# A tanh-gelu in one ScalarE instruction, and a layernorm moved from ScalarE to VectorE, in a four-layer attention and gated-MLP kernel

## The chip, the cores and the metric

The kernel runs on one core of a Trainium2 chip. The metric is device time in microseconds (us) of one execution. A core has TensorE (PE in the profile, with its weight loads as PEld), VectorE (DVE), ScalarE (ACT), GpSimd (POOL) and SyncE (SP), which starts the DMAs here. The engines run their own instruction streams and meet only at semaphores.

## The reference

The input is one sequence of 2048 tokens with 512 channels in bf16. Four residual layers follow each other: attention, gated MLP, attention, gated MLP, with the same two sets of weights.

```python
def _A_ref(x, wq, wk, wv, wo):           # 32 query heads of 16, one shared key and value head
    scores = einsum('bhqd,bkd->bhqk', q, k) * 16 ** -0.5
    o = einsum('bhqk,bkd->bhqd', softmax(scores), v)
    return o.reshape(B, S, 512) @ wo
def _B_ref(x, w_in, w_sp, b_sp, w_out):
    z = gelu_tanh(x @ w_in)              # 512 -> 1792
    z1, z2 = z[..., :896], layernorm(z[..., 896:])
    g = einsum('ts,bsf->btf', w_sp, z2) + b_sp[None, :, None]
    return (z1 * g) @ w_out
x = x + _A_ref(layernorm(x)); x = x + _B_ref(layernorm(x))
x = x + _A_ref(layernorm(x)); x = x + _B_ref(layernorm(x))
```

The gelu is the tanh approximation, and the layernorms have no gain or bias (eps 1e-5).

## The kernel before

Everything is written out by hand: `K.op(engine, function, waits, inc)` appends an instruction, or a run of matmuls, to that engine's list, so that each engine's order is the order in which Python emits. A wait becomes a wait on a semaphore count in front of the instruction.

**Prologue.** SP loads X (in four groups of tiles), the weights and `b_sp`. VectorE pads the weights (`wq_pad`, `wk_rep`, `wv_rep`), halves `w_out_r` in place (line 243, which waits for `wB`, the arrival of both MLP weights), clears `V_aug`, and then does the first layernorm.

**Attention** (`layer_A`). A loop over 512 units of four 128x512 score blocks: TensorE fills score banks (line 755), ScalarE takes three banks at a time through Exp into `P_ring` (line 774), TensorE multiplies by V, accumulating in PSUM over the 16 key tiles (line 797). Projections, transposes and the output product run as side tasks between them. The change doesn't touch this part.

**MLP** (`layer_B`). A layernorm in four chunks ends in `xnT`, 512 channels by 2048 tokens. Then comes what is called the gelu stage below: 60 items, 32 `z2` items (16 token tiles by two halves of 448 features) and then 28 `z1` items (128 features by 512 tokens). Each item is four matmuls into one of four PSUM banks (`pe_item`, lines 894 and 899) and a gelu in four steps that ping-pong between two engines:

```python
a0: ACT  ybuf  = Square(SQA * bank)            # line 932
d3: DVE  ybuf  = (ybuf + GELU_C) * bank        # line 941
a1: ACT  thbuf = Tanh(ybuf)                    # line 952
d4: DVE  out   = (thbuf + 1) * bank            # line 962, twice the gelu
```

The `LAG` loop emits them software-pipelined, one item apart. `d4` reads the bank last, so TensorE's item k waits for `d4` of item k-4. The result is twice the gelu; the halved `w_out_r` corrects this for `z1`, and 4 eps in place of eps for the normalised `z2`. For each token tile of `z2`, VectorE takes `bn_stats` of both halves (line 967) and `bn_aggr` (970), GpSimd makes the reciprocal deviation (971, 973), VectorE makes `nb2` (982), and ScalarE normalises the tile in place with Identity, scale and bias (985). `emit_norm` places the last two some six items behind.

After the stage, four passes follow: 7 groups of 16 matmuls with the transposed spatial weights (line 1050), each with two VectorE steps (1060, 1066), and 28 matmuls with `w_out_r` (1082) with the residual add (1088). The first group waits for `gelu_done`, the last item's gelu, and, matmul by matmul, for the normalised tiles.

Of the kernel before, what the change touches and what calls it, by code (L numbers as in the profile page):

```python
# [104 lines left out]
def bass_interleave_layers__grouped_kv_mqa__mixer_gmlp__prompt_kernel(  # L105
# [747 lines left out]
    def layer_B(layer_idx, x_waits):  # L853
# [69 lines left out]
        def step_a0(k):  # L923
# [4 lines left out]
            wl = [(S_pe, st["pe"][k])]  # L928
            if k >= NSLOT:
                wl.append((S_dve, st["d3"][k - NSLOT]))  # L930
                wl.append((S_act, st["a1"][k - NSLOT]))
# [3 lines left out]
        def step_d3(k):  # L935
            it = items[k]
            slot = k % NSLOT
            bk = bank32(slot)
            n = item_N(it)
            wl = [(S_act, st["a0"][k])]  # L940
            st["d3"][k] = K.op("dve", lambda e, slot=slot, bk=bk, n=n: e.scalar_tensor_tensor(  # L941
                ybuf[:, slot, 0:n], ybuf[:, slot, 0:n], GELU_C, bk[:, 0:n], op0=ALU.add, op1=ALU.mult),
                waits=wl, inc=S_dve)

        def step_a1(k):
            it = items[k]
            slot = k % NSLOT
            n = item_N(it)
            wl = [(S_dve, st["d3"][k])]
            if k >= NSLOT:  # L950
                wl.append((S_dve, st["d4"][k - NSLOT]))
            st["a1"][k] = K.op("act", lambda e, slot=slot, n=n: e.activation(  # L952
                thbuf[:, slot, 0:n], ybuf[:, slot, 0:n], ACTF.Tanh), waits=wl, inc=S_act)

        def step_d4(k):
            it = items[k]
            slot = k % NSLOT
            bk = bank32(slot)
            n = item_N(it)
            wl = [(S_act, st["a1"][k])]  # L960
# [178 lines left out]
```

## Time and profile before

| | |
|---|---|
| median of 2 runs | 2545.94 us (2543.81 to 2548.08) |
| the profiled execution's own time | 2543.34 us |
| its span from first to last instruction | 2541.3 us |
| mean granted TensorE clock | 0.658 of full speed |
| busy: PE, ACT, DVE, POOL | 1881.8, 2003.9, 577.0, 43.9 us |

Busy times are sums over the whole span, and a matmul's duration in the trace contains its pipeline, so a busy PE isn't PE at its peak; the start-to-start distance of matmuls is what counts. The span falls into six stretches: the prologue to about 52 us, attention to 1004 us, an MLP to 1280 us, attention to 2264 us, and an MLP to the end, with layernorms between them.

### The profile page before, as it was taken

To read this page: it belongs to the slowest core of one execution; us is meant where nothing else is said; L and a number is where in the kernel's file an instruction comes from. 1 tells how busy PE (TensorE), PEld (TensorE's weight loads), DVE (VectorE), ACT (ScalarE), POOL (GpSimd) and SP (SyncE) were. 2 spreads that over 40 slices of the span, in tenths; PEclk is the share of its full clock that TensorE was granted. 3 is DMA by queue.
4 is the path that set the end of the run, shared out by engine and by line. 5 is a ranking of instruction groups with operands and counts; after the bars stand their busy time and mean duration, and the time that the engine had idled before them with its cause. 6 is when DMAs were issued, how large, how long until landed. Compare 5 with 4: busy or idle time off the path is not lost.

```text
span 2541.3 us, 26575 instructions
## 1 busy us (share of the span) xinstructions
PE 1881.8 (74%) x11173; PEld 521.4 (21%) x11232; DVE 577.0 (23%) x1099; ACT 2003.9 (79%) x1639; POOL 43.9 (2%) x95
## 2 busy tenths in 40 slices
PE   2877777777777777469958777777777777764699
PEld 1223111111111111224422111111111111112244
DVE  4322100010001000794352101000100000018933
ACT  1999999999999997380039999999999999964700
POOL 0000000000000000110000000000000000001000
PEclk9998555555555555699979655555555555556999
DMA  3036000000000000201100000000000000011020
GB/s 119 1 86 164 1 1 1 1 1 1 1 1 1 1 1 1 67 1 34 34 1 1 1 1 1 1 1 1 1 1 1 1 1 1 1 33 34 1 83 18
DMA packets 60072, 43.82 MB, mean 17 GB/s; under 512 B 34864, under 2 KB 57264, under 8 KB 59952
## 3 DMA queue, kind: packets, MB, share of 16 engines
q1 hardware_dynamic: 59952, 42.11, 5.6%
q8 instruction: 88, 1.44, 0.2%
q14 instruction: 32, 0.26, 0.0%
HBM read 31.62 MB, written 10.49 MB: 17 GB/s over the span
## 4 chain that ended last, share of the span: by engine, by line
issue 34%; ACT 29%; PE 22%; DVE 14%; POOL 1%; DMA 0%; SPq 0%; another core or an unknown queue 0%; ACTq 0%
ACT P_ring L774 29%; PE ps_all L1050 8%; PE ps_all L755 4%; DVE ybuf L941 2%; PE ps_all L797 2%; PE ps_all L1082 2%; DVE oT_bf L814 2%; PE ps_all L716 2%; DVE ln_stats L277 2%; PE ps_all L664 1%; DVE z2n L962 1%; DVE z1c L962 1%; PE ps_all L303 1%; DVE st_59 L967 1%; DVE st_37 L967 1%
## 5 line engine op out<-in xcount | busy, mean ns | idle before, releaser
L774 ACT ACTIVATE P_ring<-ps_all 128x1536 bf16<-128x1536 f32 (+1 forms) x1366 | 1846.6, 1560 | 268.3 <-PE ps_all L755 267.8
L755 PE MATMUL ps_all<-qT_pad,kT_rep 32*128 32x512 bf16 x4096 | 776.6, 564 | 382.7 <-ACT P_ring L774 379.0
L797 PE MATMUL ps_all<-P_ring,V_aug 128*32 128x512 bf16 x4096 | 595.0, 570 | 2.1 <-ACT P_ring L774 2.1
L814 DVE CAST oT_bf<-ps_all 128x512 bf16<-128x512 f32 x64 | 44.3, 692 | 1422.0 <-PE ps_all L797 1421.8
L755 PEld LDWEIGHTS ps_all<-qT_pad,kT_rep 32*128 32x128 bf16 x4096 | 142.4, 98 | 991.7 <-ACT P_ring L774 936.4
L1050 PE MATMUL ps_all<-wspT,z2n 128*128 128x512 bf16 x878 | 196.8, 383 | 7.7 <-issue 6.8
L797 PEld LDWEIGHTS ps_all<-P_ring,V_aug 128*32 128x32 bf16 x4096 | 112.6, 100 | 415.8 <-issue 411.7
L932 ACT ACTIVATE ybuf<-ps_all 128x448 f32<-128x448 f32 (+1 forms) x120 | 66.0, 550 | 105.5 <-PE ps_all L894 105.5
L1050 PEld LDWEIGHTS ps_all<-wspT,z2n 128*128 128x128 bf16 x896 | 88.3, 99 | 115.3 <-issue 11.9
L894 PE MATMUL ps_all<-w_in_r,xnTB 128*128 128x448 bf16 x256 | 73.0, 424 | 40.1 <-DVE z2n L962 37.9
L941 DVE SCALAR_TENSOR_TENSOR ybuf<-ybuf,ps_all 128x448 f32<-128x448 f32 (+1 forms) x120 | 75.6, 630 | 6.4 <-ACT ybuf L932 6.4
L952 ACT ACTIVATE thbuf<-ybuf 128x448 bf16<-128x448 f32 (+1 forms) x120 | 71.2, 593 | 6.6 <-DVE ybuf L941 3.0
L664 PE MATMUL ps_all<-ident,oT_bf 128*128 128x128 bf16 x256 | 37.0, 295 | 51.3 <-DVE oT_bf L814 51.3
L899 PE MATMUL ps_all<-xnTB,w_in_r 128*128 128x512 bf16 x218 | 57.1, 382 | 18.6 <-DVE z1c L962 11.2
L1060 DVE TENSOR_TENSOR gtmp<-ps_all,bsp_bc 128x512 f32<-128x512 f32 x56 | 38.7, 692 | 124.9 <-PE ps_all L1050 124.9
L493 DVE CAST qT_pad<-ps_all 128x512 bf16<-128x512 f32 x60 | 41.5, 692 | 109.7 <-PE ps_all L488 109.7
L488 PE MATMUL ps_all<-xnTA,wq_pad 128*128 128x512 bf16 x224 | 59.8, 385 | 4.2 <-issue 1.9
L303 PE MATMUL ps_all<-ident,xnB 128*128 128x128 bf16 x128 | 15.1, 312 | 49.8 <-DVE xnB L292 49.8
L716 PE MATMUL ps_all<-wo_r,onT 128*128 128x512 bf16 x120 | 41.9, 481 | 12.8 <-DVE X L721 6.6
L277 DVE BATCH_NORM_STATS2 ln_stats<-X 128x6 f32<-128x512 bf16 x64 | 42.5, 664 | 0.2
L894 PEld LDWEIGHTS ps_all<-w_in_r,xnTB 128*128 128x128 bf16 x256 | 23.2, 109 | 89.5 <-DVE z2n L962 67.9
L282 POOL TENSOR_SCALAR ln_veps<-ln_mv 128x4 f32<-128x4 f32 (+1 forms) x12 | 2.8, 234 | 2221.0 <-DVE ln_mv L278 2221.0
(70 smaller groups left out, 720.3 us busy)
## 6 DMA issues: line engine op xcount, KB each, us to landing
wspT<-wspt_scratch SPq DMA_DIRECT2D x8, 2048.0 KB, 9.3
wsp_stage_21<-in_B_w_sp_dram SPq DMA_DIRECT2D x16, 512.0 KB, 3.9
wspt_scratch<-wspT_tile SPq DMA_DIRECT2D x16, 512.0 KB, 5.0
X<-in_A_x_dram SPq DMA_DIRECT2D x4, 512.0 KB, 5.6
out_dram<-X SPq DMA_DIRECT2D x16, 128.0 KB, 2.5
w_in_r<-in_B_w_in_dram SPq DMA_DIRECT2D x1, 1792.0 KB, 9.6
w_out_r<-in_B_w_out_dram SPq DMA_DIRECT2D x1, 896.0 KB, 10.8
wq_nat<-in_A_wq_dram SPq DMA_DIRECT2D x1, 512.0 KB, 8.3
```

Source lines behind the costliest of these rows:

```text
L277: v1 = K.op("dve", lambda e, t=t: e.bn_stats(ln_stats[:, t, :], X[:, t, :]), waits=xw_for(xw, t), inc=S_dloc)
L664: ins = e.transpose(side_bank16[:, qt * 128:(qt + 1) * 128], oT_bf[:, par, qt * 128:(qt + 1) * 128], ident[:])
L716: ins = e.matmul(side_bank32[:, 0:D], onT[:, par, c, qt * 128:(qt + 1) * 128], wo_r[:, c, :], start=(c == 0), stop=(c == 3))
L755: ins = e.matmul(bk[:, 0:QC], kT_rep[32 * j:32 * j + 32, kt * 128:(kt + 1) * 128], qT_pad[32 * j:32 * j + 32, hg, qc * QC:(qc + 1) * QC], ...
L774: return e.activation(P_ring[:, s0:s0 + n, :], bank32(b0, n).rearrange("p (k q) -> p k q", k=n)[:, :, 0:QC], ACTF.Exp, scale=DH ** -0.5)
L797: ins = e.matmul(pv_bank[32 * j:32 * j + 32, 0:QC], V_aug[:, kt, 32 * j:32 * j + 32], P_ring[:, slot, :], tile_position=(0, 32 * j), start ...
L814: v = K.op("dve", lambda e: e.tensor_copy(oT_bf[:, par, :], pv_bank[:, 0:QC]), waits=wl, inc=S_acc)
L894: ins = e.matmul(bk[:, 0:448], xnT[:, kd, t * 128:(t + 1) * 128], w_in_r[:, kd, FH + h * 448:FH + (h + 1) * 448], start=(kd == 0), stop=(k ...
L932: st["a0"][k] = K.op("act", lambda e, slot=slot, bk=bk, n=n: e.activation(ybuf[:, slot, 0:n], bk[:, 0:n], ACTF.Square, scale=SQA), waits=w ...
L941: st["d3"][k] = K.op("dve", lambda e, slot=slot, bk=bk, n=n: e.scalar_tensor_tensor(ybuf[:, slot, 0:n], ybuf[:, slot, 0:n], GELU_C, bk[:, ...
L952: st["a1"][k] = K.op("act", lambda e, slot=slot, n=n: e.activation(thbuf[:, slot, 0:n], ybuf[:, slot, 0:n], ACTF.Tanh), waits=wl, inc=S_act)
L1050: ins = e.matmul(bk[:, 0:TCW], z2n[:, sti, ft * 128:(ft + 1) * 128], wspT[:, wb, sti, :], start=(sti == 0), stop=(sti == NT - 1))
```

## The change

The four gelu steps become one ScalarE instruction that reads the PSUM bank and writes the result in bf16, with the activation function `Gelu_apprx_tanh`. TensorE's item k now waits for that instruction of item k-4. The factor of two is gone, and with it the halving of `w_out_r` in the prologue and the 4 eps. The product with `w_out_r` names `wB` in its waits. The tiles of `z2` are normalised by a VectorE `tensor_scalar` (subtract the mean, multiply by the reciprocal deviation), so that `nb2` goes. The buffers `ybuf` and `thbuf` go.

```diff
-        K.op("dve", lambda e: e.tensor_scalar(w_out_r[:], w_out_r[:], 0.5, None, op0=ALU.mult),
-             waits=[wB], inc=S_dve)
...
             if k >= NSLOT:
-                assert st["d4"][k - NSLOT] is not None
-                wl.append((S_dve, st["d4"][k - NSLOT]))
+                wl.append((S_act, st["a0"][k - NSLOT]))
...
-            st["a0"][k] = K.op("act", lambda e, slot=slot, bk=bk, n=n: e.activation(
-                ybuf[:, slot, 0:n], bk[:, 0:n], ACTF.Square, scale=SQA), waits=wl, inc=S_act)
+            st["a0"][k] = K.op("act", lambda e, bk=bk, n=n, oap=oap: e.activation(
+                oap, bk[:, 0:n], ACTF.Gelu_apprx_tanh), waits=[(S_pe, st["pe"][k])], inc=S_act)
...
-            vnb = K.op("dve", lambda e, t=t: e.scalar_tensor_tensor(nb2[:, t:t + 1], mv2[:, t, 0:1], -1.0, rstd2[:, t:t + 1],
-                                                                  op0=ALU.mult, op1=ALU.mult),
-                       waits=[(S_pool, vr2[t])], inc=S_dve)
-            vz2n[t] = K.op("act", lambda e, t=t: e.activation(z2n[:, t, :], z2n[:, t, :], ACTF.Identity,
-                                                              bias=nb2[:, t:t + 1], scale=rstd2[:, t:t + 1]),
-                            waits=[(S_dve, vnb)], inc=S_act)
+            vz2n[t] = K.op("dve", lambda e, t=t: e.tensor_scalar(z2n[:, t, :], z2n[:, t, :], mv2[:, t, 0:1], rstd2[:, t:t + 1],
+                                                                op0=ALU.subtract, op1=ALU.mult),
+                           waits=[(S_pool, vr2[t]), (S_dve, vm[t])], inc=S_dve)
+        for k in range(NIT + 2):
             while pending_norm and pending_norm[0][0] <= k:
                 emit_norm(pending_norm.pop(0)[1])
...
+            if k < NIT:
+                step_pe(k)
+            if 0 <= k - 1 < NIT:
+                step_gelu(k - 1)
+        gelu_done = (S_act, st["a0"][NIT - 1])
```

What stands in a row on the engines follows. In these rows sem13 is `S_dve`, sem14 `S_dloc` (VectorE to itself), sem15 `S_act`, sem16 `S_pe`, sem11 `S_pool`, sem17 and sem19 the score fills and the P.V products, sem5 the MLP weights; line numbers of the changed kernel are its own.

ScalarE in the first MLP, kernel before, a few items into the gelu stage:

```order
L932 ACTIVATE ybuf<-ps_all 128x448 [waits sem15,sem16]
L952 ACTIVATE thbuf<-ybuf 128x448 [waits sem13]
L932 ACTIVATE ybuf<-ps_all 128x448 [waits sem15,sem16]
L985 ACTIVATE z2n<-z2n,nb_41,rstd_40 128x896 [waits sem13]
L952 ACTIVATE thbuf<-ybuf 128x448
```

ScalarE in the changed kernel, from the last Exp of the first attention over the whole gelu stage to the first Exp of the second:

```order
L772 ACTIVATE P_ring<-ps_all 128x1024 [waits sem19,sem17]
L923 ACT_TABLE_LOAD
L923 ACTIVATE z2n<-ps_all 128x448 [waits sem16] x32
L923 ACTIVATE z1c<-ps_all 128x512 [waits sem16] x28
L772 ACT_TABLE_LOAD
L772 ACTIVATE P_ring<-ps_all 128x1536 [waits sem17] x4
```

ScalarE's stage is now 60 equal instructions that wait for TensorE alone. Four `ACT_TABLE_LOAD`s stand in the program (before each attention and each gelu stage), where before one stood at its start; the waits stand behind the loads, on the instruction that follows.

VectorE in the `z2` part of the stage, kernel before:

```order
L967 BN_STATS st_37<-z2n 128x6 [waits sem13]
L941 SCALAR_TENSOR_TENSOR ybuf<-ybuf,ps_all 128x448 [waits sem15]
L982 SCALAR_TENSOR_TENSOR nb_41<-mv_38,rstd_40 128x1 [waits sem11]
L962 SCALAR_TENSOR_TENSOR z2n<-thbuf,ps_all 128x448 [waits sem15]
L967 BN_STATS st_37<-z2n 128x6 [waits sem13]
L970 BN_AGGR mv_38<-st_37 128x2 [waits sem14]
```

The same place in the changed kernel:

```order
L930 BN_AGGR mv_36<-st_35 128x2 [waits sem14]
L927 BN_STATS st_35<-z2n 128x6 [waits sem15] x2
L930 BN_AGGR mv_36<-st_35 128x2 [waits sem14]
L942 TENSOR_SCALAR z2n<-z2n,mv_36,rstd_38 128x896 [waits sem13,sem11]
L927 BN_STATS st_35<-z2n 128x6 [waits sem15] x2
```

The four passes over each token tile's two halves are gone from between the statistics, and the normalisation of tile t stands behind the statistics of tile t+2. In the `z1` part VectorE has nothing left to do.

VectorE in the prologue, kernel before, from the last weight padding on:

```order
L220 MEMSET wv_rep 128x256
L239 COPY wv_rep<-wv_nat 128x16x16 [waits sem13]
L243 TENSOR_SCALAR w_out_r<-w_out_r 128x3584 [waits sem5]
L220 MEMSET V_aug 128x1024
L220 MEMSET V_aug 128x64 [waits sem13]
```

In the changed kernel:

```order
L220 MEMSET wv_rep 128x256
L239 COPY wv_rep<-wv_nat 128x16x16 [waits sem13]
L220 MEMSET V_aug 128x1024
L220 MEMSET V_aug 128x64 [waits sem13]
L275 BN_STATS ln_stats<-X 128x6 [waits sem0]
```

No wait for the MLP weights stands in front of the first layernorm any more.

## Rows read from the trace of the kernel before

**Rows 1.** Windows by stage: busy us per engine (count), granted clock, DMA share, GB/s.
```profile
52.50:1004.20 951.70, 728.34 (x4788) 178.85 (x4803) 106.06 (x186) 923.43 (x683) 0.00 (x0) 0.60 0.07 17
1052.26:1149.21 96.95, 65.15 (x238) 20.35 (x242) 91.40 (x184) 78.03 (x136) 12.66 (x32) 0.90 0.00 1
1149.21:1280.00 130.79, 122.82 (x549) 54.80 (x560) 50.38 (x73) 0.00 (x0) 0.00 (x0) 0.99 0.10 33
1309.00:2264.30 955.30, 729.03 (x4532) 163.28 (x4547) 83.99 (x155) 923.13 (x683) 0.00 (x0) 0.57 0.00 1
2312.39:2409.34 96.95, 64.89 (x238) 20.28 (x241) 91.42 (x184) 78.02 (x136) 12.66 (x32) 0.90 0.00 0
```

**Rows 2.** Timeline, z1 part: start, us, engine, line, shapes, idle before and releaser.
```profile
1143.51 0.58 ACT L932 ACTIVATE ybuf<-ps_all 128x512 f32<-128x512 f32 x1
...
1143.59 1.04 PE L899 MATMUL ps_all<-xnTB,w_in_r 128*128 128x512 bf16 x4 [0.16 <-DVE z1c L962]
1144.05 0.68 DVE L962 SCALAR_TENSOR_TENSOR z1c<-thbuf,ps_all 128x512 bf16<-128x512 bf16 x1
1144.17 0.63 ACT L952 ACTIVATE thbuf<-ybuf 128x512 bf16<-128x512 f32 x1
...
1144.70 0.58 ACT L932 ACTIVATE ybuf<-ps_all 128x512 f32<-128x512 f32 x1
```

**Rows 3.** Timeline, one item of the z2 part on TensorE.
```profile
1071.99 0.93 PE L894 MATMUL ps_all<-w_in_r,xnTB 128*128 128x448 bf16 x4 [0.99 <-DVE z2n L962]
```

**Rows 4.** Timeline: first weight loads at full clock in either gelu stage, then line 1050's.
```profile
1057.09 1.07 PEld L894 LDWEIGHTS ps_all<-w_in_r,xnTB 128*128 128x128 bf16 x6 [0.22 <-issue]
...
2316.47 1.51 PEld L894 LDWEIGHTS ps_all<-w_in_r,xnTB 128*128 128x128 bf16 x8 [0.22 <-issue]
...
1152.83 21.90 PEld L1050 LDWEIGHTS ps_all<-wspT,z2n 128*128 128x128 bf16 x102 [0.15 <-issue]
...
2412.25 1.82 PEld L1050 LDWEIGHTS ps_all<-wspT,z2n 128*128 128x128 bf16 x9 [0.25 <-issue]
```

**Rows 5.** Timeline, VectorE behind two neighbouring groups of 16 matmuls of line 1050.
```profile
1158.00 0.69 DVE L1060 TENSOR_TENSOR gtmp<-ps_all,bsp_bc 128x512 f32<-128x512 f32 x1 [2.03 <-PE ps_all L1050]
...
1161.45 0.69 DVE L1060 TENSOR_TENSOR gtmp<-ps_all,bsp_bc 128x512 f32<-128x512 f32 x1 [2.04 <-PE ps_all L1050]
```

**Rows 6.** Groups by line: busy us, mean ns of one, idle before and releasers.
```profile
L941 DVE SCALAR_TENSOR_TENSOR ybuf<-ybuf,ps_all 128x448 f32<-128x448 f32 (+1 forms) x120 | 75.6, 630 | 6.4 <-ACT ybuf L932 6.4
...
L952 ACT ACTIVATE thbuf<-ybuf 128x448 bf16<-128x448 f32 (+1 forms) x120 | 71.2, 593 | 6.6 <-DVE ybuf L941 3.0
...
L932 ACT ACTIVATE ybuf<-ps_all 128x448 f32<-128x448 f32 (+1 forms) x120 | 66.0, 550 | 105.5 <-PE ps_all L894 105.5
...
L962 DVE SCALAR_TENSOR_TENSOR z2n<-thbuf,ps_all 128x448 bf16<-128x448 bf16 x64 | 39.3, 613 | 0.0
L962 DVE SCALAR_TENSOR_TENSOR z1c<-thbuf,ps_all 128x512 bf16<-128x512 bf16 x56 | 38.2, 682 | 1.3 <-ACT thbuf L952 1.1
...
L967 DVE BATCH_NORM_STATS2 st_37<-z2n 128x6 f32<-128x448 bf16 x32 | 20.1, 627 | 1.1
...
L985 ACT ACTIVATE z2n<-z2n,nb_41,rstd_40 128x896 bf16<-128x896 bf16 x16 | 18.1, 1133 | 11.7 <-DVE nb_41 L982 11.6
...
L292 DVE TENSOR_SCALAR xnB<-X,ln_mv,ln_rstd 128x512 bf16<-128x512 bf16 x32 | 11.1, 409 | 11.8 <-POOL ln_rstd L284 11.8
...
L970 DVE BATCH_NORM_AGGREGATE mv_38<-st_37 128x2 f32<-128x12 f32 x16 | 3.3, 208 | 0.6
```

**Rows 7.** Timeline, prologue: the table load, and VectorE around the halving of w_out_r.
```profile
0.72 1.28 ACT L774 ACT_TABLE_LOAD   x1 [0.72 <-PEq L1124]
...
14.58 0.23 DVE L239 COPY wv_rep<-wv_nat 128x256 bf16<-128x256 bf16 x1
20.14 1.09 DVE L243 TENSOR_SCALAR w_out_r<-w_out_r 128x3584 bf16<-128x3584 bf16 x1 [5.34 <-DMA w_out_r<-in_B_w_out_dram]
21.40 0.91 DVE L220 MEMSET V_aug<- 128x1024 uint32 x1 [0.16 <-issue]
```

More of the change, by code (lines that the diff above doesn't have):

```diff
@@ L874, in layer_B @@
         rstd2 = K.sb([P, NT], FP32, lst, name="rstd2")
-        nb2 = K.sb([P, NT], FP32, lst, name="nb2")
         items = []
@@ L908, in out_ap @@
             return z1c[:, ft, tc * TCW:(tc + 1) * TCW]
-        st = {"pe": [None] * NIT, "a0": [None] * NIT, "d3": [None] * NIT, "a1": [None] * NIT, "d4": [None] * NIT}
+        st = {"pe": [None] * NIT, "a0": [None] * NIT}
         vm = [None] * NT
@@ L918, in step_pe, with step_gelu @@
             if k >= NSLOT:
[L919 to L920 removed]
+                wl.append((S_act, st["a0"][k - NSLOT]))
             st["pe"][k] = K.op("pe", lambda e, it=it, bk=bk: pe_item(e, it, bk), waits=wl, inc=S_pe)
[L923 removed]
+        def step_gelu(k):
             it = items[k]
@@ L927, in step_a0 @@
             n = item_N(it)
[L928 to L931, printed above, removed]
-            st["a0"][k] = K.op("act", lambda e, slot=slot, bk=bk, n=n: e.activation(
-                ybuf[:, slot, 0:n], bk[:, 0:n], ACTF.Square, scale=SQA), waits=wl, inc=S_act)
[L935 to L960, printed above, removed]
             oap = out_ap(it)
-            st["d4"][k] = K.op("dve", lambda e, slot=slot, bk=bk, n=n, oap=oap: e.scalar_tensor_tensor(
-                oap, thbuf[:, slot, 0:n], 1.0, bk[:, 0:n], op0=ALU.add, op1=ALU.mult),
-                waits=wl, inc=S_dve)
+            st["a0"][k] = K.op("act", lambda e, bk=bk, n=n, oap=oap: e.activation(
+                oap, bk[:, 0:n], ACTF.Gelu_apprx_tanh), waits=[(S_pe, st["pe"][k])], inc=S_act)
             if it[0] == "z2":
@@ L967, in step_d4 @@
                 v1 = K.op("dve", lambda e, t=t, h=h: e.bn_stats(st2[:, t, h, :], z2n[:, t, h * 448:(h + 1) * 448]),
-                          waits=[(S_dve, st["d4"][k])], inc=(S_dloc if h == 1 else None))
+                          waits=[(S_act, st["a0"][k])], inc=(S_dloc if h == 1 else None))
                 if h == 1:
                     vm[t] = K.op("dve", lambda e, t=t: e.bn_aggr(mv2[:, t, :], st2[:, t, :, :]), waits=[(S_dloc, v1)], inc=S_dve)
-                    vp1 = K.op("pool", lambda e, t=t: e.tensor_scalar(veps2[:, t:t + 1], mv2[:, t, 1:2], 4.0 * LN_EPS, None,
+                    vp1 = K.op("pool", lambda e, t=t: e.tensor_scalar(veps2[:, t:t + 1], mv2[:, t, 1:2], LN_EPS, None,
                                                                        op0=ALU.add), waits=[(S_dve, vm[t])], inc=S_ploc)
@@ L1008, in layer_B @@
             emit_norm(pending_norm.pop(0)[1])
-        z2n_all = (S_act, max(vz2n))
+        z2n_all = (S_dve, max(vz2n))
         wspT = K.sb([P, 2, NT, TCW], BF16, lst, name="wspT")
@@ L1048, in pe_g @@
                         if first_g:
-                            e.wait_ge(S_act.h, vz2n[sti])
+                            e.wait_ge(S_dve.h, vz2n[sti])
                         ins = e.matmul(bk[:, 0:TCW], z2n[:, sti, ft * 128:(ft + 1) * 128], wspT[:, wb, sti, :],
@@ L1054, in layer_B @@
                     wl = [w_ for w_ in wl if w_ is not z2n_all]
-                    K.waited["pe"][id(S_act)] = max(K.waited["pe"].get(id(S_act), 0), vz2n[NT - 1])
+                    K.waited["pe"][id(S_dve)] = max(K.waited["pe"].get(id(S_dve), 0), vz2n[NT - 1])
                 vg = K.op("pe", pe_g, waits=wl, inc=S_pe)
@@ L1074, in layer_B @@
                 bk = bank32(6 + yb)
-                wl = [(S_dve, vh[NF1 - 1]), w_prep]
+                wl = [(S_dve, vh[NF1 - 1]), w_prep, wB]
                 if y_bank_free[yb] is not None:
```

16 lines of the change are left out of this document (removed).

## The prediction

> **What bounds the kernel now.** I read the windows by stage first, to see which stretches the change can touch at all [rows 1]. The two attention stretches (951.7 and 955.3 us) have ScalarE busy for 923 us each, all of it Exp, and the change leaves their instructions as they are. The two gelu stages take 96.95 us each, and there VectorE is busy for 91.4, ScalarE for 78.0, and TensorE has 65 us in a duration that contains its pipeline. So VectorE bounds this stage. The stretch behind it (130.8 us) is TensorE's, at a granted clock of 0.99.
>
> The timeline shows how [rows 2]. In the z1 part one item starts every 1.19 us (ScalarE's Square at 1143.51 and again at 1144.70). VectorE's last step at 1144.05 follows the one of the item before, ScalarE's Square and Tanh (0.58 and 0.63) fill the same 1.19 us, and TensorE's four matmuls start only when VectorE releases the bank [rows 2]. In the z2 part TensorE stands idle for 0.99 us in front of an item that takes it 0.93 [rows 3], because VectorE also has the statistics to do. So the question for the change is what is late next once VectorE's two passes are gone: TensorE or ScalarE.
>
> **TensorE's own pace.** Neighbouring groups of 16 matmuls at full clock are 1161.45 - 1158.00 = 3.45 us apart [rows 5], 0.2158 us for one of 512 columns, with the wait at a group's head inside it. By columns, one of 448 takes 0.1888 us. The stage has 32 x 4 = 128 of the shorter and 28 x 4 = 112 of the longer: 24.17 + 24.17 = 48.3 us. At the start the clock is at the lower of its two levels (1.2 against 2.4 GHz): after 52 us with little on TensorE, weight loads come at the fast distance only from 1057.09 and 2316.47 on [rows 4], 4.8 and 4.1 us behind the starts of the stages [rows 1]. In that time TensorE does half of what it could, which costs 2.4 and 2.0 us.
>
> **ScalarE's pace.** An item is one activation out of PSUM. The nearest rows are Square from PSUM (mean 0.550 us) and Tanh (0.593) [rows 6]; no row shows `Gelu_apprx_tanh`. From below I take Square; from above, Square and Tanh one behind the other, 1.19 us. I take 0.58, Square's time at 512 columns [rows 2], since this too is one pass over PSUM. An item then takes TensorE 0.76 or 0.86 us and ScalarE 0.55 or 0.58, so ScalarE waits, a bank is free again more than an item before its turn (four banks), and TensorE runs without a gap.
>
> **VectorE's pace.** Per token tile two `bn_stats` (0.627), one `bn_aggr` (0.208) and the moved normalisation. For that last one, the row of line 292 is the same operation on the same types: 0.409 us for 512, hence at most 0.716 for 896 by columns [rows 6]; ScalarE's own pass over the tile took 1.133, the upper end. So 2.18 us per tile, 34.9 us for 16, from about 1055 to 1090. It is slower than TensorE's 1.51 us per tile, but TensorE no longer waits for VectorE in the stage, and 28 z1 items (24 us) lie behind the tiles. That is the cover: the first matmul of line 1050 needs the normalised tiles, and they are ready some 14 us earlier. Nothing of VectorE's is on the path.
>
> **The stage's end.** From an item's first matmul to ScalarE's start is 1144.70 - 1143.59 = 1.11 us [rows 2], that is 0.25 behind the fourth matmul's slot; then 0.58 for the gelu and 0.06 for the release: 0.9 us. A stage is 48.3 + 2.4 + 0.9 = 51.6 us, and 51.2 in the second MLP, in place of 96.95: **45.3 and 45.7 us less**.
>
> **Behind the stage.** Before, TensorE sat idle for 3.4 us while the last items went through four steps, and line 1050's first matmuls ran at the lower clock: full distance only from 1152.83 and 2412.25 on [rows 4], 3.6 and 2.9 us after their start. With a gap of 0.9 us I expect the clock to stay, which gives back half of that: **1.8 and 1.5 us**.
>
> **The prologue.** VectorE finishes the padding at 14.81 and then waits 5.3 us for the `w_out_r` transfer; `V_aug` is cleared only from 21.40 [rows 7], and the whole chain to the first Exp hangs behind that on VectorE. Without the halving it starts at 14.84: **6.6 us less**. X was loaded ahead of these weights on the same queue, so the layernorm's inputs aren't late next. SP's first loads of `w_sp` wait for the same `V_aug` and move forward too; they now run beside the rest of the weights, whose first user is the MLP, a millisecond later.
>
> **Edits at nothing.** The 4 eps, `nb2`, the buffers and the doubled `wB` change no time. The program has four table loads in place of one. The load shown takes 1.28 us and ran at 0.72 us, while its Exp waited until 52 us [rows 7, 1]: it isn't held by that wait. The order of the changed kernel has the waits behind the load in all four places, so each runs in ScalarE's idle time between the stages (over 50 us ahead of a gelu stage). I cost them at nothing; on the path the three more would cost 3 x 1.28 = 3.8 us. By the Trainium skill, "ScalarE: Activation LUTs", "What ACT_TABLE_LOAD costs", a switch of sets is about 2.66 us with its drain; as an estimate from that page, three on the path would cost 8 us, and the time would be 2453. No row here shows the drain.
>
> **The sum.** 45.3 + 45.7 + 1.8 + 1.5 + 6.6 = 100.9 us. The profiled execution took 2543.3 us, 2.0 more than its span, and would take 2442.4; the median of the runs lies 2.6 above that execution, so the forecast is **2445 us**, 4% less.
>
> **Rivals.**
> *ScalarE becomes the bound.* If the gelu costs what Square and Tanh cost together, an item takes 1.19 us at 512 and 1.07 at 448, the stage 28 x 1.19 + 32 x 1.07 + 2 = 69.6 us, and the kernel 2545.9 - 2 x 27.4 - 6.6 = 2485 us. It decides from 0.86 us per gelu on. For it: no row shows the function. Against: Square and Tanh, different functions, differ by 8% [rows 6].
>
> *The normalisation is late.* With ScalarE's 1.133 for a tile and GpSimd's whole 12.66 us of the stage [rows 1] in series, VectorE needs 16 x 2.60 + 12.7 = 54.2 us, 5 more than it has: 2445 + 10 = 2455. It decides above 3 us per tile. Against: GpSimd's part of a tile has two further tiles' statistics to hide behind.
>
> *The clock doesn't hold.* Before, the stage was granted 0.90 on average [rows 1], with TensorE idle for up to half of an item. If it stays at that, 48.3 / 0.90 = 53.7 us: 3.2 more per stage than I have, and the 3.3 us behind the stages are lost: 2455. At the lower level throughout, 95.6 us, the stage would gain nothing: 2539, within 2%. For it the Trainium skill has a rule, "TensorE: Matmul & The Clock Gate", "A second HAM failure mode: psum-queue depth-cycling": a kernel that cycles through PSUM banks leaves TensorE short idle times between groups, and its clock swings between the two levels. Against it stands the stretch of line 1050, which also cycles through its banks: 0.99 [rows 1].
>
> *Slower than before.* The mechanism is that the chip evaluates `Gelu_apprx_tanh` at the price of the steps that it replaces: 0.550 + 0.630 + 0.593 + 0.645 = 2.42 us [rows 6], all on ScalarE. A stage is then 60 x 2.42 + 1.8 = 147 us, 50 more than before, and the kernel 2545.9 + 100 - 6.6 = 2639 us. It decides from 1.64 us per gelu, three times the Square. Against it: Exp, too, takes one pass here. The Trainium skill, "ScalarE: Activation LUTs", "Step-by-step: what each stage is for", has one element per cycle and lane whatever the function; no run here shows that for this one.
>
> *The change does nothing that it says.* That is excluded: the order shows one activation per item and no VectorE pass left.
>
> **How the numbers follow.** The forecast's case 0.82, table loads on the path 0.03 (2449), the normalisation 0.03 (2455), the clock 0.05 (2455, of which 0.01 for 2539), ScalarE 0.05 (2485), slower 0.02 (2639). For the range: downward, no slow start at all gives 4.4 us more, and the two attention stretches differ by 3.6 us with the same work [rows 1], which is what a shifted start may change; with the spread of the two runs (2 us) that is 2435. Upward, the loads, the normalisation and the clock reach 2455, and with the same spreads 2460. What lies outside is ScalarE, slower and the clock's far end, under 0.1, and the tails. Two per cent, about what a measurement of this kernel can tell from no change, is 2495: faster 0.95 (it takes in most of ScalarE's case), same 0.03, slower 0.02.
>
> **What would show it.** In the changed profile: 60 activations of about 0.53 and 0.58 us per stage, ScalarE idle before each because of TensorE, line 894's matmuls 0.19 us apart without waits for a bank; the stage some 51 us long; line 1050 starting 0.9 us behind the last matmul at full clock; the last normalised tile some 14 us before that; the first Exp near 46 us; table loads inside idle time. Wrong: a gelu above 0.86 us, weight loads that wait for ScalarE, a granted clock below 0.9 in the stage, or attention stretches that changed by more than 4 us.

## The result, and the profile after

The changed kernel takes **2444.38 us** (median of 2 runs, 2443.28 to 2445.48) against 2545.94 before: a ratio of 0.9601, 95% interval 0.956 to 0.9642. The profiled execution took 2443.28 us with a span of 2441.3, that is 100.0 less span than before. The mean granted clock is 0.649.

The windows by stage of the changed kernel, with the columns of [rows 1]:

```profile
46.50:997.40 950.90, 729.30 (x4782) 180.21 (x4796) 105.46 (x185) 923.61 (x683) 0.00 (x0) 0.60 0.07 17
1047.13:1099.50 52.37, 51.48 (x242) 24.49 (x246) 27.15 (x64) 35.14 (x61) 15.02 (x32) 0.96 0.00 1
1099.50:1228.00 128.50, 120.21 (x546) 53.88 (x555) 50.69 (x75) 0.27 (x1) 0.00 (x0) 1.00 0.10 33
1257.00:2210.00 953.00, 726.85 (x4527) 163.32 (x4540) 84.01 (x154) 923.40 (x684) 0.00 (x0) 0.57 0.00 1
2259.60:2312.00 52.40, 51.47 (x244) 24.54 (x248) 27.15 (x64) 34.13 (x60) 15.02 (x32) 0.97 0.00 1
```

The second and fifth rows are the gelu stages. VectorE's work in one has fallen from 91.4 to 27.2 us and ScalarE's from 78.0 to some 34, and the stage now has TensorE's length. The attention rows have the same ScalarE work as before (923 us).

The groups by line of the changed kernel that answer to [rows 6] (shapes apart; the last number but one is the mean in ns, then the idle time before):

```profile
L889 PE MATMUL ps_all<-w_in_r,xnTB 128*128 128x448 bf16 x256 | 52.7, 371 | 1.6 <-DVE xnTB L309 1.6
L894 PE MATMUL ps_all<-xnTB,w_in_r 128*128 128x512 bf16 x218 | 48.0, 379 | 0.3
L923 ACT ACTIVATE z2n<-ps_all 128x448 bf16<-128x448 f32 x64 | 34.8, 544 | 115.8 <-PE ps_all L889 115.8
L923 ACT ACTIVATE z1c<-ps_all 128x512 bf16<-128x512 f32 x56 | 33.4, 597 | 15.0 <-PE ps_all L894 15.0
L942 DVE TENSOR_SCALAR z2n<-z2n,mv_36,rstd_38 128x896 bf16<-128x896 bf16 x16 | 7.5, 476 | 0.5 <-POOL rstd_38 L933 0.5
```

One gelu takes 0.544 or 0.597 us, and every idle time of ScalarE before one is TensorE's. TensorE itself has no idle time that ends with a bank's release: no "<-ACT" stands in its two rows, where [rows 3] showed 0.99 us of waiting for one item.

The timeline of the changed kernel, both ends of the first gelu stage and the start of the second (start, length, engine; the idle time before and its releaser in brackets):

```profile
997.45 1.28 ACT L923 ACT_TABLE_LOAD   x1
...
1047.13 6.11 PE L889 MATMUL ps_all<-w_in_r,xnTB 128*128 128x448 bf16 x20 [0.79 <-DVE xnTB L309]
...
1051.56 1.42 PEld L889 LDWEIGHTS ps_all<-w_in_r,xnTB 128*128 128x128 bf16 x8 [0.20 <-issue]
...
1078.75 0.51 DVE L942 TENSOR_SCALAR z2n<-z2n,mv_36,rstd_38 128x896 bf16<-128x896 bf16 x1 [0.46 <-POOL rstd_38 L933]
1078.88 0.60 ACT L923 ACTIVATE z1c<-ps_all 128x512 bf16<-128x512 f32 x1 [0.27 <-PE ps_all L894]
1079.74 0.60 ACT L923 ACTIVATE z1c<-ps_all 128x512 bf16<-128x512 f32 x1 [0.27 <-PE ps_all L894]
...
1097.87 0.60 ACT L923 ACTIVATE z1c<-ps_all 128x512 bf16<-128x512 f32 x1 [0.27 <-PE ps_all L894]
1098.49 1.28 ACT L772 ACT_TABLE_LOAD   x1
1098.54 4.44 PEld L999 LDWEIGHTS ps_all<-wspT,z2n 128*128 128x128 bf16 x22 [1.20 <-issue]
1098.57 4.69 PE L999 MATMUL ps_all<-wspT,z2n 128*128 128x512 bf16 x21 [0.73 <-issue]
1102.22 0.69 DVE L1009 TENSOR_TENSOR gtmp<-ps_all,bsp_bc 128x512 f32<-128x512 f32 x1 [22.96 <-PE ps_all L999]
...
2263.30 1.61 PEld L889 LDWEIGHTS ps_all<-w_in_r,xnTB 128*128 128x128 bf16 x9 [0.18 <-issue]
```

One z1 item starts every 0.86 us, 1.19 in [rows 2]. The stage runs from 1047.13 to line 999's first matmul at 1098.57, 51.44 us. Line 999 (1050 before) runs at full clock from its first weight load, where [rows 4] had it 3.6 us later. Its first VectorE step follows 3.65 us behind the first matmul. The last tile is normalised at 1079.26, 19 us before line 999 needs it. Both table loads stand in ScalarE's idle time. The second stage lasts from 2259.64 to 2310.70, 51.06 us.

VectorE in the prologue and the first Exp, in the timeline of the changed kernel, for [rows 7]:

```profile
14.64 0.23 DVE L239 COPY wv_rep<-wv_nat 128x256 bf16<-128x256 bf16 x1
15.02 0.91 DVE L220 MEMSET V_aug<- 128x1024 uint32 x1 [0.16 <-issue]
...
46.95 1.45 ACT L772 ACTIVATE P_ring<-ps_all 128x1536 bf16<-128x1536 f32 x1 [44.95 <-PE ps_all L753]
```

### The profile page after: what moved, and what is told of

Its sections match the earlier page's. It is cut to its first block, busy times and chain, and to the rows that moved or that the text cites. A ratio compares the mean times of both kernels' runs of the same rounds, so it can differ in the third digit from the quotient of the medians.

```text
span 2441.3 us, 26105 instructions
## 1 busy us (share of the span) xinstructions
PE 1850.9 (76%) x11173; PEld 530.3 (22%) x11232; DVE 447.6 (18%) x858; ACT 1920.4 (79%) x1490; POOL 48.6 (2%) x95
## 4 chain that ended last, share of the span: by engine, by line
issue 35%; ACT 29%; PE 26%; DVE 7%; POOL 1%; DMA 0%; SPq 0%; another core or an unknown queue 0%; ACTq 0%; DVEq 0%
ACT P_ring L772 29%; PE ps_all L999 8%; PE ps_all L753 4%; PE ps_all L795 2%; PE ps_all L889 2%; PE ps_all L1031 2%; PE ps_all L894 2%; DVE oT_bf L812 2%; PE ps_all L714 2%; DVE ln_stats L275 2%; PE ps_all L662 1%; PE ps_all L301 1%; DVE X L719 1%; PE ps_all L696 1%; POOL ln_rstd L282 1%
## 5 line engine op out<-in xcount | busy, mean ns | idle before, releaser
L923 ACT ACTIVATE z2n<-ps_all 128x448 bf16<-128x448 f32 x64 | 34.8, 544 | 115.8 <-PE ps_all L889 115.8
L889 PE MATMUL ps_all<-w_in_r,xnTB 128*128 128x448 bf16 x256 | 52.7, 371 | 1.6 <-DVE xnTB L309 1.6
L894 PE MATMUL ps_all<-xnTB,w_in_r 128*128 128x512 bf16 x218 | 48.0, 379 | 0.3
L923 ACT ACTIVATE z1c<-ps_all 128x512 bf16<-128x512 f32 x56 | 33.4, 597 | 15.0 <-PE ps_all L894 15.0
L662 PEld LDWEIGHTS ps_all<-ident,oT_bf 128*128 128x128 bf16 x256 | 21.2, 127 | 81.8 <-DVE oT_bf L812 81.8
L383 PE MATMUL ps_all<-xnTA,wk_rep 128*128 128x512 bf16 x26 | 9.3, 484 | 34.2 <-DVE xnTA L309 34.2
```

Of the source, the lines that this page charges most:

```text
L662: ins = e.transpose(side_bank16[:, qt * 128:(qt + 1) * 128], oT_bf[:, par, qt * 128:(qt + 1) * 128], ident[:])
L889: ins = e.matmul(bk[:, 0:448], xnT[:, kd, t * 128:(t + 1) * 128], w_in_r[:, kd, FH + h * 448:FH + (h + 1) * 448], start=(kd == 0), stop=(k ...
L894: ins = e.matmul(bk[:, 0:TCW], w_in_r[:, kd, ft * 128:(ft + 1) * 128], xnT[:, kd, tc * TCW:(tc + 1) * TCW], start=(kd == 0), stop=(kd == K ...
L923: st["a0"][k] = K.op("act", lambda e, bk=bk, n=n, oap=oap: e.activation(oap, bk[:, 0:n], ACTF.Gelu_apprx_tanh), waits=[(S_pe, st["pe"][k]) ...
```

## The experiments

The kernel before, run beside each, had medians of 2544.1 to 2545.1 us. A stage runs from the first matmul with `w_in_r` to the first one with `wspT`. "Changed" is the changed kernel, 51.44 and 51.06 us per stage.

**What bounds the stage before: the normalisation alone moved (e3).** The kernel before with only this edit:

```diff
-            vz2n[t] = K.op("act", lambda e, t=t: e.activation(z2n[:, t, :], z2n[:, t, :], ACTF.Identity,
...
+            vz2n[t] = K.op("dve", lambda e, t=t: e.tensor_scalar(z2n[:, t, :], z2n[:, t, :], mv2[:, t, 0:1], rstd2[:, t:t + 1],
```

> The kernel before with its four gelu steps, and the second layernorm's tiles normalised on VectorE: the other half of the change alone. Theory (VectorE's work bounds the stage before): about 0.4 us more and 0.1 less of VectorE per tile, 16 x 0.3 = 5 us more per stage, 102 us in place of 96.95, about 2556. Rival (the relay between ScalarE and VectorE bounds it, and ScalarE loses 1.13 us per tile): the stage gets shorter, by 5 us or more, 2536 or less.

Measured: 2554.55 us (2551.64 to 2556.65), ratio 1.0038 (1.0025 to 1.0051); stages 102.36 and 101.96 against 96.95. The window over the first stage shows VectorE (the third pair) busy for nearly all of it:

```profile
1052.00:1156.00 104.00, 70.81 (x242) 21.98 (x246) 97.71 (x185) 64.04 (x120) 12.70 (x32) 0.84 0.00 0
```

The stage grew by 5.4 us as VectorE's work in it did by 5.7 (of the 97.71, 0.66 is a copy of the layernorm just ahead of the stage), although ScalarE lost 14: VectorE bound the z2 part, where the normalisation stands. The run doesn't decide the z1 part, which it leaves alone: there both engines were near full before (VectorE 26.5 and ScalarE 25.4 of the 27 us from 1118 to 1145). The second half of the change, alone, makes the kernel slower by 0.4%.

**The other half alone: gelu in one step, normalisation left on ScalarE (e2).** The changed kernel, with `nb2` again.

```diff
-            vz2n[t] = K.op("dve", lambda e, t=t: e.tensor_scalar(z2n[:, t, :], z2n[:, t, :], mv2[:, t, 0:1], rstd2[:, t:t + 1],
...
+            vz2n[t] = K.op("act", lambda e, t=t: e.activation(z2n[:, t, :], z2n[:, t, :], ACTF.Identity,
```

> The changed kernel, with the second layernorm's tiles normalised on ScalarE again (Identity, 1.13 us per tile). Theory: ScalarE then needs 2 x 0.54 + 1.13, about 2.1 us per tile with overlap, against TensorE's 1.51, so that it bounds the z2 part: 16 x 0.6 = 9 to 10 us more per stage, about 2463. Rival (ScalarE's idle time and the four banks take it up): under 2 us per stage, at most 2448. Second rival (Identity needs another table): two loads of 1.28 us per tile, over 40 us more per stage.

Measured: 2484.86 us (2483.68 to 2485.77), ratio 0.9765 (0.9749 to 0.9782); stages 71.84 and 71.51, 20.4 more each, twice what was expected. ScalarE's added work is 16 x 1.133 = 18 us, and in the first row of the changed stage above it had 52.4 - 35.1 = 17 us idle. The next two runs ask what the rest is.

**The same, with the normalisation 12 items behind (e11).**

```diff
-                    pending_norm.append((k + 6, t))
+                    pending_norm.append((k + 12, t))
```

> The changed kernel with the normalisation left to ScalarE as before (Identity, nb2 by VectorE), each placed 12 items behind its statistics in place of 6. If what cost 20 us per stage in the earlier version was the relay in order (ScalarE waits for nb, which stands behind statistics that wait for gelus), then with the wait gone only ScalarE's work counts: 0.85 us for two gelus and 1.13 for the normalisation against TensorE's 1.51 per tile, some ten tiles inside the z2 part: 5 to 8 us more per stage than the changed kernel, stage 57 to 60, 2456 to 2461. If it is the work on ScalarE and its wait on VectorE anyhow: 71 per stage, 2484 again.

Measured: 2477.13 us (2476.15 to 2480.13), ratio 0.9739 (0.9724 to 0.9754); the first stage 68.15. A miss (2456 to 2461 was expected): the greater distance takes away 7.7 us of e2's 40.5, and the wait only where no statistics are left. One tile of the z2 part in its timeline, and two rows of the z1 part:

```profile
1071.93 1.13 ACT L946 ACTIVATE z2n<-z2n,nb,rstd 128x896 bf16<-128x896 bf16 x1 [1.05 <-DVE nb L943]
...
1072.97 0.96 ACT L924 ACTIVATE z2n<-ps_all 128x448 bf16<-128x448 f32 x2
1073.52 1.15 DVE L928 BATCH_NORM_STATS2 st<-z2n 128x6 f32<-128x448 bf16 x2 [1.63 <-ACT z2n L924]
...
1074.71 0.21 DVE L931 BATCH_NORM_AGGREGATE mv<-st 128x2 f32<-128x12 f32 x1
1074.84 0.11 DVE L943 SCALAR_TENSOR_TENSOR nb<-mv,rstd 128x1 f32<-128x1 f32 x1
1074.98 1.13 ACT L946 ACTIVATE z2n<-z2n,nb,rstd 128x896 bf16<-128x896 bf16 x1 [1.05 <-DVE nb L943]
...
1092.22 1.13 ACT L946 ACTIVATE z2n<-z2n,nb,rstd 128x896 bf16<-128x896 bf16 x1
1093.25 1.08 ACT L924 ACTIVATE z1c<-ps_all 128x512 bf16<-128x512 f32 x2
```

The `nb` of an old tile, whose inputs have long been there, stands in VectorE's order behind the statistics of the two gelus that ScalarE has just made; ScalarE's Identity waits for `nb`, and the next gelus stand behind Identity. The two engines run in turn, 3.05 us per tile, with 12 items of distance as with 6 (e2). In the z1 part the same Identity waits for nothing.

**The same, with nb made ahead (e13).** VectorE's `nb` six items earlier than the Identity.

```diff
+                    pending_nb.append((k + 6, t))
...
+            while pending_nb and pending_nb[0][0] <= k:
+                emit_nb(pending_nb.pop(0)[1])
```

> The version with the normalisation on ScalarE placed 12 items behind, with one difference: VectorE makes nb of a tile six items earlier than ScalarE's Identity needs it, so that it stands ahead of, not behind, the statistics that wait for ScalarE's last gelus. The relay's account: the wait of 1.05 us in front of each Identity goes; a tile in the z2 part takes ScalarE 0.95 + 1.04 = 2.0 us against TensorE's 1.51, one in the z1 part 2.0 against 1.73, as the z1 part of the earlier version already showed; ten tiles in the one and six in the other give 10 x 0.47 + 6 x 0.25 = 6 us more per stage than the changed kernel: stage 57 to 58, 2456 (2453 to 2460). If the Identity's own work on ScalarE or another wait cost the 16 us of that version: 2477 again.

Measured: 2451.71 us (2449.27 to 2454.28), ratio 0.9636 (0.962 to 0.9652); the first stage 55.49, 4.1 more than changed where 6 were expected. ScalarE in its timeline:

```profile
1061.85 1.14 ACT L951 ACTIVATE z2n<-z2n,nb,rstd 128x896 bf16<-128x896 bf16 x1
...
1062.88 0.98 ACT L924 ACTIVATE z2n<-ps_all 128x448 bf16<-128x448 f32 x2
...
1063.72 1.15 ACT L951 ACTIVATE z2n<-z2n,nb,rstd 128x896 bf16<-128x896 bf16 x1
```

The wait is gone, and a tile takes 1.87 us, not the 2.0 expected. Of e2's 40.5 us, 8 went with the distance (e11), 25 with the order of `nb` on VectorE, and some 7 are left for ScalarE's work. So the moved normalisation is worth 7 us with the best order tried here, and 40 with the order that the kernel before had.

**Does ScalarE bound the changed stage? A small extra activation per item (e5).** 32 columns more, 0.20 us by its duration.

```diff
+            K.op("act", lambda e, bk=bk, n=n, slot=slot: e.activation(
+                gscr[:, slot, 0:32], bk[:, 0:32], ACTF.Gelu_apprx_tanh), waits=[(S_pe, st["pe"][k])])
```

> The changed kernel with one extra gelu of 32 columns per item into a scratch tile, about 0.2 us of ScalarE. Theory (TensorE bounds): 0.54 + 0.2 and 0.60 + 0.2 us stay under TensorE's 0.757 and 0.863 per item, so the stage stays within 1 us of 51.3 and the time within 3 us of the changed kernel's. Rival (ScalarE's time or latency adds to each item): 0.2 x 60 = 12 us more per stage, about 2468.

Measured: 2442.49 us (2442.14 to 2444.79), ratio 0.9601 (0.9588 to 0.9614); stages 51.72 and 51.62, 0.3 and 0.6 more. The gelu behind the extra one starts 0.09 us after it, so by start distances 60 x 0.09 = 5.4 us were added per stage, and not 12; nearly all of it is hidden, and the kernel isn't slower. ScalarE doesn't bound the stage; with no wait in TensorE's rows either, TensorE does.

**Every gelu twice (e4).** The same edit with all columns.

```diff
+                gscr[:, slot, 0:n], bk[:, 0:n], ACTF.Gelu_apprx_tanh), waits=[(S_pe, st["pe"][k])])
```

> The changed kernel with every gelu computed twice, the first into a scratch tile that nobody reads. Theory (TensorE bounds the stage, ScalarE has 0.2 to 0.26 us of idle time per item): ScalarE, about 1.0 and 1.12 us per item, becomes the bound, 32 x 1.0 + 28 x 1.12 + 2.5 = 66 us per stage in place of 51.3, about 2474. Rival (ScalarE's work is hidden altogether): the stage stays under 53 us. Rival (ScalarE was the bound already): 0.54 and 0.60 us more per item, the stage near 85 us, about 2511.

Measured: 2459.18 us (2457.99 to 2459.55), ratio 0.9664 (0.965 to 0.9678); stages 58.46 and 58.08. ScalarE is the bound here, but at much less than two durations. Its timeline, gelus back to back:

```profile
1069.60 1.07 ACT L924 ACTIVATE gscr<-ps_all 128x448 bf16<-128x448 f32 x1
...
1070.03 1.09 ACT L926 ACTIVATE z2n<-ps_all 128x448 bf16<-128x448 f32 x1
...
1070.45 1.10 ACT L924 ACTIVATE gscr<-ps_all 128x448 bf16<-128x448 f32 x1
```

One starts every 0.425 us, though a gelu that stands alone lasts 0.544: they overlap by 0.12. (The durations shown here grow, to 2.02 us at the stage's end, while the starts stay evenly apart; they aren't the price of a gelu.) The expectation priced the item by durations.

**Two PSUM banks in place of four (e9).**

```diff
-NSLOT = 4
+NSLOT = 2
```

> The changed kernel with two PSUM banks in place of four. Theory: TensorE waits for the gelu two items back; one round of matmuls, 0.25 us to ScalarE, gelu and release is 1.6 us for two items at 448 columns and 1.77 at 512, 0.80 and 0.89 per item in place of 0.757 and 0.863, and the clock stays: about 2 us more per stage, 2449. Rival (short idle times between groups make the clock swing): the granted clock of the stage falls below 0.90 and the stage takes 57 us or more, 2456 or more.

Measured: 2444.98 us (2444.59 to 2445.63), ratio 0.9609 (0.9596 to 0.9622); both stages 52.31, 0.9 and 1.3 more. The weight loads now show the bank's release, and the clock of the stage's window (the last number but two) stays; the window takes in 1.7 us ahead of the stage, and over the stage alone it is 0.96, as in the changed kernel:

```profile
1061.79 0.49 PEld L889 LDWEIGHTS ps_all<-w_in_r,xnTB 128*128 128x128 bf16 x4 [0.32 <-ACT z2n L923]
...
1047.00:1100.00 53.00, 52.21 (x249) 20.18 (x246) 28.59 (x66) 33.48 (x59) 14.97 (x32) 0.94 0.00 1
```

**The halving, first attempt: on GpSimd (e1).** The kernel before, with line 243 moved to GpSimd, behind the first attention's work there, waiting for `wB` alone.

```diff
-        K.op("dve", lambda e: e.tensor_scalar(w_out_r[:], w_out_r[:], 0.5, None, op0=ALU.mult),
...
+    v_half = K.op("pool", lambda e: e.tensor_scalar(w_out_r[:], w_out_r[:], 0.5, None, op0=ALU.mult),
+                  waits=[wB], inc=S_pool)
```

> The kernel before, with the halving of w_out_r moved from VectorE in the prologue to GpSimd behind the first attention; all else as before. Theory (the wait for w_out_r is on the chain to the first Exp): first Exp at about 47 us in place of 52.9, the gelu stages 96.95 us as before, the time 6 us (0.24%) less, about 2540. Rival (another arrival, X or the attention weights, is late next): first Exp above 50 us, under 3 us less.

Measured: 2547.49 us (2545.73 to 2548.33), ratio 1.0009 (0.9999 to 1.0018). A miss. The chain came 6.4 us earlier at first, and lost it in one place of the timeline:

```profile
34.44 13.04 DVE L290 TENSOR_SCALAR xnA<-X,ln_mv,ln_rstd 128x512 bf16<-128x512 bf16 x12 [2.78 <-POOL ln_rstd L282]
...
34.49 9.30 POOL L1096 TENSOR_SCALAR w_out_r<-w_out_r 128x3584 bf16<-128x3584 bf16 x1
```

VectorE's twelve steps took 13.04 us, 3.97 in the changed kernel, while GpSimd's halving ran beside them; the first of them alone took 9.49, the others 0.40 each. The run therefore says nothing on the prologue's term, and e10 takes its place.

**The halving on an idle engine (e10).** The kernel before, with the halving as a ScalarE Identity behind the first attention's last Exp.

```diff
-        K.op("dve", lambda e: e.tensor_scalar(w_out_r[:], w_out_r[:], 0.5, None, op0=ALU.mult),
-             waits=[wB], inc=S_dve)
...
     xw = layer_A(0, xw, do_wspt=True)
+    v_half = K.op("act", lambda e: e.activation(w_out_r[:], w_out_r[:], ACTF.Identity, scale=0.5),
+                  waits=[wB], inc=S_act)
```

> The kernel before, with the halving of w_out_r taken out of VectorE's prologue and done by one ScalarE Identity (scale 0.5) right behind the last Exp of the first attention, where ScalarE is idle for 50 us. Nothing else is changed. My account of the prologue: VectorE clears V_aug at about 15.0 in place of 21.4, the first Exp starts at about 47 in place of 53, and the kernel takes 6 us less: 2538 beside 2544 (2535 to 2541, the attention stretches varying by 2). The rival from the halving on GpSimd, that whatever is taken out there comes back before the first Exp: no change, 2544.

Measured: 2539.07 us (2536.76 to 2541.47) against 2545.14, ratio 0.9977 (0.9967 to 0.9987): 6.1 us less. In its timeline the chain is the changed kernel's:

```profile
14.92 0.91 DVE L220 MEMSET V_aug<- 128x1024 uint32 x1 [0.16 <-issue]
...
34.38 3.96 DVE L290 TENSOR_SCALAR xnA<-X,ln_mv,ln_rstd 128x512 bf16<-128x512 bf16 x12 [2.78 <-POOL ln_rstd L282]
...
46.41 4.13 ACT L772 ACTIVATE P_ring<-ps_all 128x1536 bf16<-128x1536 f32 x3 [44.41 <-PE ps_all L753]
```

**The slow start of the stage (e6).** The changed kernel with 18 matmuls without use ahead of the last layernorm chunk's transposes, so that TensorE isn't idle there.

```diff
+            if c == NCH - 1:
+                K.op("pe", pe_warm, waits=[wB], inc=S_pe)
```

> The changed kernel with 18 matmuls of 512 columns into an unused bank in front of the last chunk's transposes of each MLP's layernorm, so that TensorE isn't idle before the stage. Theory (the stage's first 4 to 5 us run at the lower clock for want of work before): the first items run at full distance, 0.19 us per matmul, and the stage is 1.5 to 2.4 us shorter: about 2440. Rival (the extra matmuls hold up the last transposes, or the clock falls again in the gap behind them): no gain, or up to 2 us per MLP lost.

Measured: 2438.1 us (2436.42 to 2441.22), ratio 0.9583 (0.957 to 0.9596); both stages 49.29, 2.15 and 1.77 less. The last chunk's transposes ran faster too, so that from the last Exp to the first `wspT` matmul the gain is 2.8 and 2.4. The full distance stands from the stage's first weight load on:

```profile
1044.88 7.11 PEld L896 LDWEIGHTS ps_all<-w_in_r,xnTB 128*128 128x128 bf16 x39 [0.96 <-DVE xnTB L309]
```

**What is left beside the stage: items issued chunk by chunk (e7).** Of the 50 us from the last Exp to the stage, some 32 are a layernorm on VectorE, in which TensorE does little. Here the eight z2 items of a chunk follow that chunk's transposes, the layernorm uses banks 4 and 5, and VectorE does the z2 statistics behind the layernorm.

```diff
+            if k < 2 * NT and k % (2 * CT) == 0:
+                c = k // (2 * CT)
+                vl, _ = ln_direct_chunk(c, x_waits, xnB, NT, xnT, [4, 5], bfree)
+                xnT_chunk[c] = (S_dve, vl)
```

> The changed kernel, with the z2 items of a chunk of four token tiles issued as soon as that chunk's layernorm is transposed, in place of all 16 tiles first; VectorE does its statistics and normalisation behind the whole layernorm, and the layernorm uses two other banks. Theory (with the gelu on ScalarE, TensorE and ScalarE are idle for the 32 us of the layernorm, and VectorE in the stage, so that the two can overlap): z2's 24 us move into the layernorm, VectorE's 27 us of statistics beside the z1 part: 20 us less per MLP, about 2404. Rival (the items run at the lower clock in short bursts and hold up the transposes behind them, or VectorE's statistics end late): under 10 us less per MLP, 2425 or more.

Measured: 2408.83 us (2407.6 to 2410.03), ratio 0.9467 (0.9454 to 0.948). From the last Exp to the first `wspT` matmul it takes 83.0 us in place of 101.1 and 100.7, some 18 less where 20 were expected. The first chunk shows what the sum of the expectation had left out and its rival had named, in its timeline:

```profile
1023.62 8.49 PE L887 MATMUL ps_all<-w_in_r,xnTB 128*128 128x448 bf16 x32 [0.79 <-DVE xnTB L309]
...
1032.59 0.69 DVE L309 COPY xnTB<-ps_all 128x1024 bf16<-128x1024 bf16 x1 [2.98 <-PE ps_all L301]
```

Its 32 matmuls begin at the lower clock, and the second chunk's transposes wait behind them, and VectorE for these.

**Both together (e12).** e7, with 13 of e6's matmuls ahead of the first chunk's transposes.

```diff
+                if c == 0:
+                    K.op("pe", pe_warm, waits=[wB] + list(xw_all(x_waits)), inc=S_pe)
```

> Both additions together: the gelu stage fed chunk by chunk of the layernorm, and 13 matmuls without use ahead of the first chunk's transposes (from the last addition to X on, 5.5 us in which TensorE has nothing to do). The first chunk's 32 matmuls then run at full clock (6.2 us in place of 8.5), and the second chunk's transposes come 2 to 2.5 us sooner: 2 to 2.5 us less per MLP than the overlapped version's 2408.8, so 2404 (2402 to 2407). If VectorE's layernorm chain and not TensorE sets the pace of the first chunks, no change: 2409.

Measured: **2401.94 us** (2401.07 to 2403.11), ratio 0.944 (0.9427 to 0.9453), the fastest version here, at the lower edge of what was expected. The same two rows in its timeline, and the first `wspT` matmuls of both MLPs:

```profile
1022.27 6.23 PE L887 MATMUL ps_all<-w_in_r,xnTB 128*128 128x448 bf16 x32 [0.79 <-DVE xnTB L309]
...
1028.98 1.29 DVE L309 COPY xnTB<-ps_all 128x1024 bf16<-128x1024 bf16 x2 [0.72 <-PE ps_all L301]
...
1077.58 24.33 PE L1017 MATMUL ps_all<-wspT,z2n 128*128 128x512 bf16 x110 [0.73 <-issue]
...
2268.47 24.33 PE L1017 MATMUL ps_all<-wspT,z2n 128*128 128x512 bf16 x110 [0.73 <-issue]
```

From the last Exp to the first `wspT` matmul it takes 80.1 us in both MLPs, 2.9 less than e7 (2.0 to 2.5 were expected), and 21.0 and 20.6 less than changed. The other 1.1 of the 6.9 us that it gains on e7 are a balance of small differences elsewhere (in the two profiles 2.8 less in the attention stretches, 1.5 more ahead of the second), which no run explains.

## Why the prediction was right, step by step

The forecast was 2445 and the median 2444.4, and the sum was right by its parts. That the two lie 0.6 apart is luck: the span fell by 100.0 us where 100.9 were summed, the runs' median lies 1.1 above the profiled execution where 2.6 were added, and the two medians rest on two runs each, 2 and 4 us apart.

| step of the prediction | predicted | measured |
|---|---|---|
| first gelu stage | 51.6, 45.3 less | 51.44, 45.5 less |
| second gelu stage | 51.2, 45.7 less | 51.06, 45.9 less |
| behind the first stage | 1.8 less | 1.7 less, 1.15 of it given back |
| behind the second stage | 1.5 less | 1.4 less |
| prologue | 6.6 less | 6.4 on VectorE, 6.0 at the first Exp |
| attention stretches | unchanged | first 0.8 more, second 1.6 less |

*TensorE's pace* was right: an item every 0.86 us at 512 columns. That it is the bound is shown by two runs: a small extra activation per item costs 0.3 and 0.6 us per stage (e5), and two banks cost only 0.9 and 1.3 (e9). *VectorE's bound before* is shown by e3 for the z2 part; for the z1 part, where ScalarE was nearly as full, it was argued from busy times. *ScalarE's pace*: the gelu was taken at 0.58 for 512 columns and is 0.597; the shorter at 0.55, and is 0.544. The rivals with a gelu of 1.19 or 2.42 us are excluded by that.

*ScalarE as the bound* was the rival nearest to hand, and its turning point was mis-sized: "from 0.86 us per gelu on" compares TensorE's distance between items with a duration. What counts is the distance at which ScalarE can start activations, 0.425 for a duration of 0.544 (e4). With two gelus per item, 1.09 us by durations, the z2 part ran at 0.85. With that overlap a single gelu would turn the stage at some 0.98 us for 512 columns (an estimate, 0.86 + 0.12).

*The moved normalisation* was the least certain of the costs that could be bounded: at most 0.716 was allowed, 0.476 is the mean. GpSimd's two steps stayed hidden but for 0.5 us, and the cover is 19 us, not 14. The prediction counted only what the move takes on VectorE. What it saves on ScalarE it didn't price, and this is the larger part of its worth: 40 us in the order that stood there (e2), 7 in the best one tried (e13).

*The slow start* was predicted at 2.4 and 2.0 us from the first weight loads at full distance. They come 4.4 and 3.7 us behind the stage's start now, half of which is 2.2 and 1.8; taking the slow start away gave 2.15 and 1.77 (e6).

*Behind the stage* TensorE kept its clock through the 0.73 us gap, as predicted. In e4 the gap was 2.93 us, and the clock was lost: the first VectorE step came 5.34 us behind line 999's first matmul, in place of 3.65. But the length of the gap, by which alone the prediction went, isn't the whole reason. In e3 it was 3.38 us in both MLPs, as in the kernel before; behind the second the step came after 5.34 us, behind the first after 3.65, at the full clock:

```profile
1155.07 7.28 PE L1047 MATMUL ps_all<-wspT,z2n 128*128 128x512 bf16 x33 [3.38 <-issue]
...
1158.72 0.69 DVE L1057 TENSOR_TENSOR gtmp<-ps_all,bsp_bc 128x512 f32<-128x512 f32 x1 [3.75 <-PE ps_all L1047]
```

What made the difference there stays open. Of the first MLP's 1.7 us, 1.15 were lost again just ahead of the second attention: VectorE's steps there are 52.33 us earlier than before up to the layernorm, and the casts of the query projection 51.2 to 51.3, since the projections ran longer at the lower clock. Why the clock rose later there wasn't tried.

*The prologue*: e10 gives the halving's removal alone 6.1 us. The 6.6 left out the 0.16 us that VectorE takes ahead of `V_aug` in either kernel. In the changed kernel 0.4 of the 6.4 is lost in the query projection (2.63 us, 2.26 before and 2.20 in e10), again by the clock: its weight loads come at the fast distance from the sixth of eight on, before from the fourth.

*Clock that doesn't hold.* In the two stages the granted clock is 0.96 and 0.97, the start included, and 1.00 behind it. In the kernel before it did not hold, which its mean of 0.90 hides: in the z2 part, with TensorE waiting up to 0.99 us per item [rows 3], it fell twice to the lower level for 6.8 us and rose again. The first two rows are the kernel before, the third is the changed kernel:

```profile
1074.20:1081.00 6.80, 5.83 (x15) 1.38 (x13) 6.63 (x16) 5.25 (x11) 1.58 (x4) 0.50 0.00 0
1094.70:1101.50 6.80, 5.77 (x15) 1.29 (x12) 6.63 (x16) 5.30 (x9) 1.58 (x4) 0.50 0.02 4
...
1051.60:1098.50 46.90, 46.08 (x226) 22.18 (x227) 25.86 (x62) 33.05 (x59) 15.02 (x32) 1.00 0.00 1
```

VectorE, the third pair, was busy for nearly all of these two stretches. The Trainium skill's rule for cycling PSUM banks ("TensorE: Matmul & The Clock Gate", "A second HAM failure mode: psum-queue depth-cycling") describes the kernel before; it doesn't describe the changed kernel, whose four banks leave TensorE no such waits, nor e9, where two banks leave waits of up to 0.32 us on the weight loads. So this rival was a real one: the clock fell in a stage with long waits on TensorE and held without them. That the waits are the cause is argued from these runs, and none was made to show it. (At the lower level throughout, the rival's stage is twice 48.3, so 96.6 and not 95.6.)

*Table loads at nothing*: each takes 1.28 us, and the two behind attention start 0.02 us behind the end of the last Exp (at 997.43 and 2209.95), some 50 us before the first gelu. By the Trainium skill, "ScalarE: Activation LUTs", "What ACT_TABLE_LOAD costs", a switch comes to some 2.66 us with its drain; here nothing waits for it, so that no run shows the drain.

## What to carry to other kernels

When one engine's passes are taken out of a loop, ask which engine's start-to-start distance is next, and compare distances with distances: back to back, an activation costs less than its duration. What an engine needs from another belongs, in that other engine's order, ahead of whatever waits for the first; a greater distance alone gave 8 of the 33 us that lay in it here. Once TensorE bounds a stage, the next gain is its idle time around the stage: feeding it as soon as a chunk is there, and with something to do ahead of that, gave another 42 us here.
